# A gated linear attention with a max-out layer behind it: weights in contiguous blocks, groups of two tiles, row moves from another queue, and a new order of the opening

## The chip, the cores and the metric

The kernel runs on one core of a Trainium2 chip. Times are device microseconds of one execution. The time of the kernel before in its first three runs was 207.36 us (median; 206.71 to 207.45). A profile is one such execution recorded by the hardware profiler; its span is from the first to the last instruction.

Ratios are the mean time of one kernel's fast runs over that of the other's of the same rounds, so not quite the ratio of the medians that are quoted beside them. The medians are of all executions and can hold slow ones: two of four in e2s_sync_moves, one each in e2_pool_moves, b2_weights and e7_o_later, and of the kernel before five of seven in the rounds of e6 and e7 (median 209.14; its two fast ones took 207.27 and 205.84). Intervals are 95%. Where an interval lies wholly below 0.98 the text calls the kernel faster; the record classes six of these runs (e2s, b2, e3, e5, e6, e7) as unclear all the same, without a reason.

## The reference

```python
# q, k, v, f_logit: (B=4, H=8, S=768, D=48) float32
f = 1 / (1 + exp(-f_logit))
for t in range(S):                                  # a gated linear attention
    state = f[:, :, t, :, None] * state + k_t (x) v_t
    y[:, :, t] = q_t . state
x = y.transpose(0, 2, 1, 3).reshape(B * S, H * D)   # 3072 x 384
out = maximum(x @ w1, x @ w2) @ w_out               # d_ff = 1024
```

## The kernel before

The sequence is cut into 6 chunks of 128 positions. A *tile* is one chunk of one batch, so there are 24 tiles; each passes through the stages E (logs of the gates), C and X (cumulated sums and their exponentials), M (k and q scaled by them, on GpSimd), V, T (transposes), A (masked products), Y (output and state). The layer behind uses max(a, b) = b + relu(a - b): with wd = w1 - w2 and M2 = w2 @ w_out, the output is relu(x @ wd) @ w_out + x @ M2. Eight *h* pieces make relu(x @ wd) for a group of tiles, and one *o* piece per tile the output.

The attention leaves x transposed, in a layout of two halves of 64 partitions: 48 rows of a head, then 16 rows to be filled from a fourth plane, so that 384 rows fit into three planes of 128. The fill is a DMA from SBUF to SBUF, the *row move*. The rows of w1 and w2 must be in the same order; before, the load puts them there, in pieces of 48 and 16 partitions.

```python
def load(n):                                   # four loads of 192 KB a tile
    ...
        nc.sync.dma_start(out=t, in_=src[b, :, sl, :].rearrange("h p d -> p h d"))

def load_rows(dst, w):                         # rows of w1, w2 straight into their places
    hd = w.rearrange("(h d) f -> d h f", d=D)
    nc.sync.dma_start(out=dst[0:D, :, :], in_=hd[:, 0:6:2, :])
    nc.sync.dma_start(out=dst[DP:DP + D, :, :], in_=hd[:, 1:6:2, :])
    for r in range(2):
        h = 6 + r
        rows = w[h * D:(h + 1) * D, :].rearrange("(k i) f -> i k f", k=KT)
        nc.sync.dma_start(out=dst[r * DP + D:(r + 1) * DP, :, :], in_=rows)
...
def stage_Y_act(n):
    ...
    nc.scalar.copy(xT[c][:, :, b * C:(b + 1) * C], ys.pop(n))
    if b == B - 1:                             # once in four tiles: six row moves
        x = xT[c]
        for r in range(2):
            for i in range(KT):
                nc.sync.dma_start(out=x[r * DP + D:(r + 1) * DP, i, :],
                                  in_=x[r * DP + 16 * i:r * DP + 16 * (i + 1), KT, :])
...
for n in range(5):                             # five tiles ahead
    load(n)
    if n == B - 1:
        load_rows(w2_f, moe_w2); load_rows(w1_f, moe_w1); ...   # then w_out
...                                            # slot n, one for each tile:
    load(n + 5); E(n + 3); A(n); Y(n - 1); C, X, M (n + 2)
    ...                                        # weights are prepared in slots 3, 4, 5
    piece_d; V, T (n + 1); piece_d; piece_o    # two h pieces and one o, if there are any
```

In the profiles the row moves of the sync queue are issued behind the loads that precede them in the code (in e2s_sync_moves below at 85.09 us, after four loads issued from 81.8 to 85.0). Names in the profiles: PEld is TensorE's weight loading, DVE VectorE, POOL GpSimd, SPq and ACTq the issuing of DMAs on the sync queue and on ScalarE's; ft is the loaded gates, kp and qp the scaled k and q, trp and trs their transposes, at_e and at_o the products of A, gT is relu(x @ wd), and wdn and m2n are wd and M2 before they are permuted.

Of the kernel before, what the change touches and what calls it, by code (L numbers as in the profile page):

```python
# [16 lines left out]
def kernel(  # L17
# [17 lines left out]
    nc = tc.nc  # L35
# [9 lines left out]
    NT = B * C  # L45
# [17 lines left out]
    loaded = {}  # L63

    def load(n):
        c, b = divmod(n, B)
        sl = slice(c * C, (c + 1) * C)
        tiles = {}
        for nm, src in (("f", f_logit), ("k", k), ("q", q), ("v", v)):
            t = inp.tile([C, H, D], F32, name=f"{nm}t", tag=f"{nm}t")  # L70
            nc.sync.dma_start(out=t, in_=src[b, :, sl, :].rearrange("h p d -> p h d"))  # L71
            tiles[nm] = t
        loaded[n] = tiles
# [5 lines left out]
    def load_rows(dst, w):  # L79

        hd = w.rearrange("(h d) f -> d h f", d=D)
        nc.sync.dma_start(out=dst[0:D, :, :], in_=hd[:, 0:6:2, :])
        nc.sync.dma_start(out=dst[DP:DP + D, :, :], in_=hd[:, 1:6:2, :])
        for r in range(2):
            h = 6 + r
            rows = w[h * D:(h + 1) * D, :].rearrange("(k i) f -> i k f", k=KT)
            nc.sync.dma_start(out=dst[r * DP + D:(r + 1) * DP, :, :], in_=rows)
# [7 lines left out]
    nc.gpsimd.memset(ones_col, 1.0)  # L95
    NB = 3
    padded = {}
    for nm in ("ell", "qp", "kp", "vb"):
        padded[nm] = []
        for i in range(NB):  # L100
            t = consts.tile([C, H, DP], BF16, name=f"{nm}{i}")
            nc.gpsimd.memset(t, 0.0)
            padded[nm].append(t)
    ut4 = consts.tile([C, NP, C], BF16, name="ut4")
    for j in range(NP):
        nc.gpsimd.tensor_copy(ut4[:, j, :], ut)

    wd = consts.tile([C, KT, d_ff], BF16, name="wd")
    w2b = consts.tile([C, KT, d_ff], BF16, name="w2b")
    wo = consts.tile([C, FG, HD], BF16, name="wo")  # L110
    w2T = consts.tile([C, FG, HD], BF16, name="w2T")
# [128 lines left out]
    def stage_Y_act(n):  # L240
        c, b = divmod(n, B)
        if b == 0:
            xT[c] = xpool.tile([C, NP, NT], BF16, name="xT", tag="xT", bufs=3)
        nc.scalar.copy(xT[c][:, :, b * C:(b + 1) * C], ys.pop(n))  # L244
        if b == B - 1:
            x = xT[c]
            for r in range(2):
                for i in range(KT):
                    nc.sync.dma_start(out=x[r * DP + D:(r + 1) * DP, i, :],  # L249
                                      in_=x[r * DP + 16 * i:r * DP + 16 * (i + 1), KT, :])  # L250


    def piece_d(g, ff):
        if ff == 0:
            gT[g] = xpool.tile([C, FG, NT], BF16, name="gT", tag="gT")
        ps = bank("h")
        for kt in range(KT):
            nc.tensor.matmul(out=ps, lhsT=wd[:, kt, ff * C:(ff + 1) * C], rhs=xT[g][:, kt, :],  # L258
                             start=(kt == 0), stop=(kt == KT - 1))
        nc.scalar.activation(gT[g][:, ff, :], ps, AF.Relu)  # L260

    def piece_o(g, b):
# [7 lines left out]
        return ps  # L270

    def finish_o(g, b, ps):
        ob = opool.tile([C, HD], F32, name="ob", tag="ob")
        nc.vector.tensor_copy(ob, ps)  # L274
        row = b * S + g * C
        nc.sync.dma_start(out=out[row:row + C, :], in_=ob)

    def prep_weights_1():
        nc.vector.tensor_copy(w2b, w2_f)
        nc.gpsimd.tensor_sub(wd, w1_f, w2_f)  # L280
        nc.vector.tensor_copy(wo, wo_f)

    def prep_weights_2():
        for kt in range(KT):
            ps = bank("w2t", BF16).rearrange("p (f r) -> p f r", f=FG)
# [5 lines left out]
    def prep_weights_3():  # L291
        for kt in range(KT):
            ps = bank("m2p")[:, 0:HD]
# [3 lines left out]
            nc.scalar.copy(m2[:, kt, :], ps)  # L297
# [3 lines left out]
    first = {3: prep_weights_1, 4: prep_weights_2, 5: prep_weights_3}  # L301
    queue = []
    for n in range(AHEAD):
        load(n)
        if n == B - 1:
# [84 lines left out]
```

## Time and profile before

| | before |
|---|---|
| time, span | 207.36, 204.9 us |
| TensorE busy (PE) | 141.6 us, 69% |
| first h | 72.8 us |
| last o ends | 201.4 us |
| a full slot (attention, two h, one o) | 5.03 us |

### The profile page before, as it was taken

The page shows a single profiled execution, that of the slowest core. Times are in us where ns is not written, and L with a number is a line of the kernel's source. Part 1 is how long each engine was busy: PE and PEld are TensorE (multiplying, and loading weights), DVE is VectorE, ACT ScalarE, POOL GpSimd, SP SyncE. Part 2 cuts the span into 40 slices and gives each one's busy share as a digit, 9 for nine tenths or more (in the row PEclk, how much of TensorE's full clock was granted, in tenths as well). Part 3 has the DMA queues.
Part 4 walks back from the last instruction along what each step waited for, and adds up shares of the span by engine and source line. Part 5 has one row for each costly group of instructions (what it writes and reads, how often), then busy time and mean ns, then how long its engine had stood idle before and what let it go on. Part 6 is the DMA issues. An engine that isn't in the chain of part 4 may idle for free.

```text
span 204.9 us, 3795 instructions
## 1 busy us (share of the span) xinstructions
PE 141.6 (69%) x1452; PEld 85.7 (42%) x1472; DVE 81.6 (40%) x145; ACT 87.6 (43%) x196; POOL 72.3 (35%) x90
## 2 busy tenths in 40 slices
PE   0257300004464999929999699995999999959993
PEld 0134200002353655614666356663566655515551
DVE  0047500001978346531555426662566554111221
ACT  4333000017552479823666346664466544313400
POOL 8754000003599508640455505554055530000000
PEclk9999999999999799975999979997999999979999
DMA  6999999999999499958699589795891111111122
GB/s 126 189 186 191 162 163 168 228 242 198 186 187 187 72 187 185 171 97 172 141 176 217 116 167 179 150 224 107 168 196 45 58 42 40 45 55 38 55 95 80
DMA packets 106402, 29.15 MB, mean 142 GB/s; under 512 B 100944, under 2 KB 105616, under 8 KB 106384
## 3 DMA queue, kind: packets, MB, share of 16 engines
q1 hardware_dynamic: 106384, 28.91, 77.7%
q8 instruction: 11, 0.18, 0.4%
q14 instruction: 7, 0.06, 0.1%
HBM read 23.59 MB, written 4.72 MB: 138 GB/s over the span
## 4 chain that ended last, share of the span: by engine, by line
PE 52%; issue 19%; SPq 9%; DMA 8%; DVE 5%; ACT 3%; POOL 2%; DVEq 0%; POOLq 0%
PE h L258 15%; PE o L268 13%; PE o L265 5%; SPq L249 5%; PE trp L160 4%; SPq L71 4%; DMA xT<-xT 4%; PE at_e L178 3%; PE y L205 3%; PE y L200 3%; PE m2p L295 2%; DMA ft<-in_f_logit_dram 2%; DMA qt<-in_q_dram 2%; PE cum L127 2%; DVE vb L153 1%
## 5 line engine op out<-in xcount | busy, mean ns | idle before, releaser
L258 PE MATMUL h<-xT,wd 128*128 128x512 bf16 x124 | 41.7, 413 | 12.2 <-DMA xT<-xT 10.3
L260 ACT ACTIVATE gT<-h 128x512 bf16<-128x512 f32 x48 | 28.9, 603 | 31.2 <-PE h L258 30.7
L147 POOL TENSOR_TENSOR kp<-kt,f_inv 128x384 bf16<-128x384 f32 x24 | 24.9, 1037 | 39.6 <-ACT f_inv L140 36.0
L168 DVE COPY trs<-trp 128x1024 bf16<-128x1024 bf16 x24 | 16.6, 691 | 54.3 <-PE trp L160 54.3
L268 PE MATMUL o<-wo,gT 128*128 128x384 bf16 x192 | 35.1, 326 | 0.0
L274 DVE COPY ob<-o 128x384 f32<-128x384 f32 x24 | 13.4, 558 | 52.4 <-PE o L268 52.4
L127 PE MATMUL cum<-ell,ut 128*128 128x384 bf16 x24 | 9.3, 389 | 32.4 <-ACT ell L121 32.4
L120 ACT ACTIVATE tmp_e<-ft 128x384 f32<-128x384 f32 x24 | 12.4, 518 | 42.2 <-DMA ft<-in_f_logit_dram 42.2
L235 POOL TENSOR_TENSOR state<-tmp_s,f_last 128x256 bf16<-128x256 f32 x16 | 10.5, 658 | 53.2 <-DVE tmp_s L234 47.3
L244 ACT CAST xT<-y 128x512 bf16<-128x512 f32 x24 | 14.0, 582 | 29.4 <-PE y L205 29.4
L268 PEld LDWEIGHTS <-gT 128*128 128x128 bf16 x192 | 18.9, 98 | 12.7 <-issue 0.5
L149 POOL TENSOR_TENSOR qp<-qt,f_dec 128x384 bf16<-128x384 f32 x24 | 24.0, 1000 | 0.0
L258 PEld LDWEIGHTS <-wd 128*128 128x128 bf16 x144 | 12.6, 102 | 22.1 <-DMA xT<-xT 14.0
L130 PEld LDWEIGHTS <-ell 128*128 128x128 bf16 x96 | 6.5, 104 | 33.3 <-issue 32.3
L186 DVE TENSOR_TENSOR at_m<-at_e,ut 128x512 bf16<-128x512 f32 x24 | 16.4, 685 | 5.7 <-PE at_o L178 5.7
L178 PE MATMUL at_e<-trs 48*128 48x128 bf16 x96 | 10.7, 240 | 10.7 <-DVE trs L168 10.3
L265 PE MATMUL o<-m,xT 128*128 128x384 bf16 x72 | 16.7, 344 | 0.0
L186 DVE TENSOR_TENSOR at_m<-at_o,ut 128x512 bf16<-128x512 f32 x24 | 16.3, 681 | 0.0
L153 DVE CAST vb<-vt 128x384 bf16<-128x384 f32 x24 | 12.0, 498 | 7.1 <-DMA vt<-in_v_dram 7.1
L178 PEld LDWEIGHTS <-trs 48*128 48x128 bf16 x192 | 6.1, 102 | 18.4 <-DVE trs L168 13.7
L160 PE MATMUL trp<-ident,kp 128*128 128x128 bf16 x96 | 11.1, 249 | 3.1 <-POOL kp L147 3.1
L121 ACT ACTIVATE ell<-tmp_e 128x384 bf16<-128x384 f32 x24 | 12.6, 523 | 0.9
(42 smaller groups left out, 168.5 us busy)
## 6 DMA issues: line engine op xcount, KB each, us to landing
ft<-in_f_logit_dram SPq DMA_DIRECT2D x24, 192.0 KB, 4.0
kt<-in_k_dram SPq DMA_DIRECT2D x24, 192.0 KB, 4.4
qt<-in_q_dram SPq DMA_DIRECT2D x24, 192.0 KB, 4.4
vt<-in_v_dram SPq DMA_DIRECT2D x24, 192.0 KB, 4.2
out_dram<-ob SPq DMA_DIRECT2D x24, 192.0 KB, 2.0
w_f<-in_moe_w_dram SPq DMA_DIRECT2D x4, 576.0 KB, 13.2
wo_f<-in_moe_w_out_dram SPq DMA_DIRECT2D x1, 1536.0 KB, 20.8
w_f<-in_moe_w_dram SPq DMA_DIRECT2D x4, 192.0 KB, 16.0
```

The lines of the kernel that those rows point to most:

```text
L147: nc.gpsimd.tensor_mul(padded["kp"][n % NB][:, :, 0:D], loaded[n]["k"], f_inv.rearrange("p (h d) -> p h d", h=H))
L149: nc.gpsimd.tensor_mul(padded["qp"][n % NB][:, :, 0:D], loaded[n]["q"], f_dec.rearrange("p (h d) -> p h d", h=H))
L153: nc.vector.tensor_copy(padded["vb"][n % NB][:, :, 0:D], loaded[n]["v"])
L160: nc.tensor.transpose(out=ps[:, x, j, :], in_=src[:, 2 * j:2 * j + 2, :].rearrange("p h e -> p (h e)"), identity=ident)
L168: nc.vector.tensor_copy(t, ps)
L178: nc.tensor.matmul(out=ps[r][:, j, :], lhsT=t[rows, 0, j, :], rhs=t[rows, 1, j, :], start=True, stop=True)
L186: nc.vector.tensor_mul(m[:, r], ps[r], ut4)
L244: nc.scalar.copy(xT[c][:, :, b * C:(b + 1) * C], ys.pop(n))
L258: nc.tensor.matmul(out=ps, lhsT=wd[:, kt, ff * C:(ff + 1) * C], rhs=xT[g][:, kt, :], start=(kt == 0), stop=(kt == KT - 1))
L260: nc.scalar.activation(gT[g][:, ff, :], ps, AF.Relu)
L265: nc.tensor.matmul(out=ps, lhsT=xT[g][:, kt, b * C:(b + 1) * C], rhs=m2[:, kt, :], start=(kt == 0), stop=False)
L268: nc.tensor.matmul(out=ps, lhsT=gT[g][:, ff, b * C:(b + 1) * C], rhs=wo[:, ff, :], start=False, stop=(ff == FG - 1))
```

## The change

It has four main parts. (1) w1 and w2 are loaded as they lie, 128 rows at a time, and put in order afterwards by matmuls with 0/1 matrices: 14 for wd, 7 for M2. (2) The layer works on groups of two tiles instead of four, so h matmuls have 256 columns instead of 512 and twice the count. (3) The row moves are two DMAs a group instead of six, issued from ScalarE's queue. (4) The opening has a new order: attention of two tiles, then all weights, then the first group's layer, then the loop; in the loop loads are three tiles ahead instead of five. The full diff also moves the set-up memsets from GpSimd to VectorE and gives xT four buffers instead of three.

```diff
-    def load_rows(dst, w):  ...
+    def load_weights():
+        for dst, w in ((w2_f, moe_w2), (w1_f, moe_w1)):
+            for kt in range(KT):
+                nc.sync.dma_start(out=dst[:, kt, :], in_=w[kt * C:(kt + 1) * C, :])
+        ...                                        # w_out in two halves
+    perm = consts.tile([C, KT, KT, 2, DP], BF16, name="perm")     # built by GpSimd
...
-                for i in range(KT):
-                    nc.sync.dma_start(out=x[r * DP + D:(r + 1) * DP, i, :], ...)
+                rows = x[r * DP:r * DP + D, KT, :]
+                nc.scalar.dma_start(out=x[r * DP + D:(r + 1) * DP, 0:KT, :], in_=rows)
...
+    def weights_w2():
+        for kt in range(KT):
+            nc.scalar.copy(w2b[:, kt, :], w2_f[:, kt, :])
+            ...                                    # 8 transposes, copy to w2T by DVE
+    def weights_wd():
+        for kt in range(KT):
+            nc.vector.tensor_sub(wdn[:, kt, :], w1_f[:, kt, :], w2_f[:, kt, :])
+        ...                                        # 14 matmuls with perm, 6 copies
+    def weights_m2():
+        for h in range(2):
+            nc.scalar.copy(wo[:, half, :], wo_f[:, half, :])
+        ...                                        # 24 matmuls, 7 with perm, 6 copies
...
+    load(0); load(1); load(2, "f"); load(3, "f")
+    load_weights()
+    load(2, "kqv"); load(3, "kqv"); load(4)
+    ...                                            # tiles 0 and 1 up to Y; E, C of 2 and 3
+    weights_w2()
+    weights_wd()
+    do("M", 2)
+    for fp in range(FG // 2):
+        piece_d(0, fp)
+    weights_m2()
+    do("VT", 2); do("M", 3); do("E", 4)
...
+        if 5 <= n + 3 < n_tiles:                   # slot n, from n = 2
+            load(n + 3)
+        A(n); Y(n - 1); C, M (n + 2); piece_d; V, T (n + 1); piece_d; E(n + 3); piece_o
```

More of the change, by code (lines that the diff above doesn't have):

```diff
@@ L44 @@
     KT = HD // C
-    NT = B * C
+    GB = 2
+    NT = GB * C
     n_tiles = nch * B
@@ L60, with load @@
     nc.scalar.preload_act_table_set("natural_log_exp_and_others")
-    loaded = {}
-    def load(n):
+    loaded = {n: {} for n in range(n_tiles)}
+    sources = {"f": f_logit, "k": k, "q": q, "v": v}
+    def load(n, names="fkqv"):
         c, b = divmod(n, B)
-        sl = slice(c * C, (c + 1) * C)
-        tiles = {}
-        for nm, src in (("f", f_logit), ("k", k), ("q", q), ("v", v)):
+        for nm in names:
             t = inp.tile([C, H, D], F32, name=f"{nm}t", tag=f"{nm}t")
-            nc.sync.dma_start(out=t, in_=src[b, :, sl, :].rearrange("h p d -> p h d"))
-            tiles[nm] = t
-        loaded[n] = tiles
+            nc.sync.dma_start(out=t, in_=sources[nm][b, :, c * C:(c + 1) * C, :].rearrange("h p d -> p h d"))
+            loaded[n][nm] = t
     w1_f = wst.tile([C, KT, d_ff], F32, name="w1_f")
@@ L77 @@
     wo_f = wst.tile([C, FG, HD], F32, name="wo_f")
-    def load_rows(dst, w):
-        hd = w.rearrange("(h d) f -> d h f", d=D)
-        nc.sync.dma_start(out=dst[0:D, :, :], in_=hd[:, 0:6:2, :])
-        nc.sync.dma_start(out=dst[DP:DP + D, :, :], in_=hd[:, 1:6:2, :])
-        for r in range(2):
-            h = 6 + r
-            rows = w[h * D:(h + 1) * D, :].rearrange("(k i) f -> i k f", k=KT)
-            nc.sync.dma_start(out=dst[r * DP + D:(r + 1) * DP, :, :], in_=rows)
+    def load_weights():
[3 more added lines that the diff above has]
+        for h in range(2):
+            half = slice(h * FG // 2, (h + 1) * FG // 2)
+            nc.sync.dma_start(out=wo_f[:, half, :],
+                              in_=moe_w_out.rearrange("(j p) m -> p j m", p=C)[:, half, :])
     ut = consts.tile([C, C], BF16, name="ut")
@@ L94 @@
     ones_col = consts.tile([C, 1], BF16, name="ones_col")
-    nc.gpsimd.memset(ones_col, 1.0)
+    nc.vector.memset(ones_col, 1.0)
     NB = 3
     padded = {}
-    for nm in ("ell", "qp", "kp", "vb"):
+    for nm in ("ell", "kp", "qp", "vb"):
         padded[nm] = []
@@ L101 @@
             t = consts.tile([C, H, DP], BF16, name=f"{nm}{i}")
-            nc.gpsimd.memset(t, 0.0)
+            nc.vector.memset(t, 0.0)
             padded[nm].append(t)
@@ L105, with build_perm, sources_of @@
     for j in range(NP):
-        nc.gpsimd.tensor_copy(ut4[:, j, :], ut)
+        nc.vector.tensor_copy(ut4[:, j, :], ut)
+    perm = consts.tile([C, KT, KT, 2, DP], BF16, name="perm")
+    def build_perm():
+        nc.gpsimd.memset(perm, 0.0)
+        for kt in range(KT):
+            for cols, pattern, base in (
+                    (slice(0, D), [[-2 * D, KT], [-D, 2], [-1, D]], kt * C),
+                    (slice(D, DP), [[-1, KT], [-D, 2], [-KT, DP - D]], kt * C - 2 * KT * D)):
+                part = perm[:, kt, :, :, cols]
+                nc.gpsimd.affine_select(out=part, in_=part, compare_op=mybir.AluOpType.not_equal,
+                                        fill=1.0, base=base, pattern=pattern, channel_multiplier=1)
+    def sources_of(i):
+        return sorted({2 * D * i // C, (2 * D * (i + 1) - 1) // C, KT - 1})
+    w2b = wst.tile([C, KT, d_ff], BF16, name="w2b")
+    wdn = wst.tile([C, KT, d_ff], BF16, name="wdn")
+    w2T = wst.tile([C, FG, HD], BF16, name="w2T")
+    m2n = wst.tile([C, KT, HD], BF16, name="m2n")
     wd = consts.tile([C, KT, d_ff], BF16, name="wd")
-    w2b = consts.tile([C, KT, d_ff], BF16, name="w2b")
     wo = consts.tile([C, FG, HD], BF16, name="wo")
-    w2T = consts.tile([C, FG, HD], BF16, name="w2T")
     m2 = consts.tile([C, KT, HD], BF16, name="m2")
@@ L240, in stage_Y_act, with piece_d @@
     def stage_Y_act(n):
-        c, b = divmod(n, B)
+        g, b = divmod(n, GB)
         if b == 0:
-            xT[c] = xpool.tile([C, NP, NT], BF16, name="xT", tag="xT", bufs=3)
-        nc.scalar.copy(xT[c][:, :, b * C:(b + 1) * C], ys.pop(n))
-        if b == B - 1:
-            x = xT[c]
+            xT[g] = xpool.tile([C, NP, NT], BF16, name="xT", tag="xT", bufs=4)
+        nc.scalar.copy(xT[g][:, :, b * C:(b + 1) * C], ys.pop(n))
+        if b == GB - 1:
+            x = xT[g]
             for r in range(2):
-                for i in range(KT):
-                    nc.sync.dma_start(out=x[r * DP + D:(r + 1) * DP, i, :],
-                                      in_=x[r * DP + 16 * i:r * DP + 16 * (i + 1), KT, :])
-    def piece_d(g, ff):
-        if ff == 0:
-            gT[g] = xpool.tile([C, FG, NT], BF16, name="gT", tag="gT")
-        ps = bank("h")
-        for kt in range(KT):
-            nc.tensor.matmul(out=ps, lhsT=wd[:, kt, ff * C:(ff + 1) * C], rhs=xT[g][:, kt, :],
-                             start=(kt == 0), stop=(kt == KT - 1))
-        nc.scalar.activation(gT[g][:, ff, :], ps, AF.Relu)
+                rows = x[r * DP:r * DP + D, KT, :]
+                nc.scalar.dma_start(out=x[r * DP + D:(r + 1) * DP, 0:KT, :], in_=rows)
+    def piece_d(g, fp):
+        if fp == 0:
+            gT[g] = xpool.tile([C, FG, NT], BF16, name="gT", tag="gT", bufs=3)
+        ps = bank("h").rearrange("p (f t) -> p f t", f=2)
+        for f in range(2):
+            ff = 2 * fp + f
+            for kt in range(KT):
+                nc.tensor.matmul(out=ps[:, f, :], lhsT=wd[:, kt, ff * C:(ff + 1) * C],
+                                 rhs=xT[g][:, kt, :], start=(kt == 0), stop=(kt == KT - 1))
+        nc.scalar.activation(gT[g][:, 2 * fp:2 * fp + 2, :], ps, AF.Relu)
     def piece_o(g, b):
@@ L269, in piece_o @@
                              start=False, stop=(ff == FG - 1))
-        return ps
-    def finish_o(g, b, ps):
         ob = opool.tile([C, HD], F32, name="ob", tag="ob")
         nc.vector.tensor_copy(ob, ps)
-        row = b * S + g * C
+        c, bb = divmod(g * GB + b, B)
+        row = bb * S + c * C
         nc.sync.dma_start(out=out[row:row + C, :], in_=ob)
-    def prep_weights_1():
-        nc.vector.tensor_copy(w2b, w2_f)
-        nc.gpsimd.tensor_sub(wd, w1_f, w2_f)
-        nc.vector.tensor_copy(wo, wo_f)
-    def prep_weights_2():
+    def weights_w2():
         for kt in range(KT):
+            nc.scalar.copy(w2b[:, kt, :], w2_f[:, kt, :])
             ps = bank("w2t", BF16).rearrange("p (f r) -> p f r", f=FG)
@@ L289, in prep_weights_2 @@
             nc.vector.tensor_copy(w2T[:, :, kt * C:(kt + 1) * C], ps)
-    def prep_weights_3():
+    def weights_wd():
         for kt in range(KT):
-            ps = bank("m2p")[:, 0:HD]
+            nc.vector.tensor_sub(wdn[:, kt, :], w1_f[:, kt, :], w2_f[:, kt, :])
+        for h in range(2):
+            half = slice(h * d_ff // 2, (h + 1) * d_ff // 2)
+            for i in range(KT):
+                ps = bank("wdp")
+                ks = sources_of(i)
+                for kt in ks:
+                    nc.tensor.matmul(out=ps, lhsT=perm[:, kt, i].rearrange("p r d -> p (r d)"),
+                                     rhs=wdn[:, kt, half], start=(kt == ks[0]), stop=(kt == ks[-1]))
+                if i == 1:
+                    nc.vector.tensor_copy(wd[:, i, half], ps)
+                else:
+                    nc.scalar.copy(wd[:, i, half], ps)
+    def weights_m2():
+        for h in range(2):
+            half = slice(h * FG // 2, (h + 1) * FG // 2)
+            nc.scalar.copy(wo[:, half, :], wo_f[:, half, :])
+        for kt in range(KT):
+            ps = bank("m2n")[:, 0:HD]
             for ff in range(FG):
@@ L296, in prep_weights_3, with do, next_piece @@
                                  start=(ff == 0), stop=(ff == FG - 1))
-            nc.scalar.copy(m2[:, kt, :], ps)
-    AHEAD = 5
-    first = {3: prep_weights_1, 4: prep_weights_2, 5: prep_weights_3}
-    queue = []
-    for n in range(AHEAD):
-        load(n)
-        if n == B - 1:
-            load_rows(w2_f, moe_w2)
-            load_rows(w1_f, moe_w1)
-            nc.sync.dma_start(out=wo_f, in_=moe_w_out.rearrange("(j p) m -> p j m", p=C))
-    def ok(n):
-        return 0 <= n < n_tiles
-    def next_piece(n, kind):
+            nc.scalar.copy(m2n[:, kt, :], ps)
+        for i in range(KT):
+            ps = bank("m2p")[:, 0:HD]
+            ks = sources_of(i)
+            for kt in ks:
+                nc.tensor.matmul(out=ps, lhsT=perm[:, kt, i].rearrange("p r d -> p (r d)"),
+                                 rhs=m2n[:, kt, :], start=(kt == ks[0]), stop=(kt == ks[-1]))
+            nc.vector.tensor_copy(m2[:, i, :], ps)
+    AHEAD = 5
+    done = set()
+    steps = {
+        "E": stage_E, "M": stage_M, "V": stage_V,
+        "C": lambda n: (stage_C(n), stage_X(n)),
+        "T": lambda n: (stage_T_pe(n), stage_T_dve(n)),
+        "A": lambda n: (stage_A_pe(n), stage_A_dve(n)),
+        "Y": lambda n: (stage_Y_pe(n), stage_Y_act(n), stage_D_pe(n), stage_D_dve(n)),
+    }
+    def do(names, n):
+        for nm in names:
+            if 0 <= n < n_tiles and (nm, n) not in done:
+                done.add((nm, n))
+                steps[nm](n)
+    load(0)
+    load(1)
+    load(2, "f")
+    load(3, "f")
+    load_weights()
+    load(2, "kqv")
+    load(3, "kqv")
+    load(4)
+    do("E", 0)
+    do("E", 1)
+    for n in range(2):
+        do("CM", n)
+    for n in range(2):
+        do("VT", n)
+    build_perm()
+    do("A", 0)
+    do("A", 1)
+    for n in range(2):
+        do("E", n + 2)
+    for n in range(2):
+        do("Y", n)
+    for n in range(2, 4):
+        do("C", n)
+    weights_w2()
[4 more added lines that the diff above has]
+    weights_m2()
+    do("VT", 2)
+    do("M", 3)
+    do("E", 4)
+    queue = [("o", 0, b) for b in range(GB)]
+    def next_piece(kind):
         for i, (kd, g, j) in enumerate(queue):
@@ L317, in next_piece @@
                 if kd == "o" and any(p[0] == "d" and p[1] == g for p in queue):
-                    return None
-                return queue.pop(i)
-        return None
-    slot = -3
-    while slot < n_tiles + 2 or queue:
-        n = slot
-        if n % B == 1 and 4 < n <= n_tiles + 1:
-            g = (n - 5) // B
-            queue += [("d", g, ff) for ff in range(FG)] + [("o", g, b) for b in range(B)]
-        if ok(n + AHEAD) and n + AHEAD >= AHEAD:
-            load(n + AHEAD)
-        if ok(n + 3):
-            stage_E(n + 3)
-        if ok(n):
-            stage_A_pe(n)
-            stage_A_dve(n)
-        if ok(n - 1):
-            stage_Y_pe(n - 1)
-            stage_Y_act(n - 1)
-            stage_D_pe(n - 1)
-            stage_D_dve(n - 1)
-        if ok(n + 2):
-            stage_C(n + 2)
-            stage_X(n + 2)
-            stage_M(n + 2)
-        if n in first:
-            first[n]()
-        p = next_piece(n, "d")
-        if p:
-            piece_d(*p[1:])
-        if ok(n + 1):
-            stage_V(n + 1)
-            stage_T_pe(n + 1)
-            stage_T_dve(n + 1)
-        p = next_piece(n, "d")
-        if p:
-            piece_d(*p[1:])
-        p = next_piece(n, "o")
-        if p:
-            finish_o(*p[1:], piece_o(*p[1:]))
-        slot += 1
+                    return
+                queue.pop(i)
+                (piece_d if kind == "d" else piece_o)(g, j)
+                return
+    n = 2
+    while n < n_tiles + 2 or queue:
+        if n % GB == 1 and 3 < n <= n_tiles + 1:
+            g = (n - 3) // GB
+            queue += [("d", g, fp) for fp in range(FG // 2)] + [("o", g, b) for b in range(GB)]
+        if 5 <= n + 3 < n_tiles:
+            load(n + 3)
+        do("A", n)
+        do("Y", n - 1)
+        do("C", n + 2)
+        do("M", n + 2)
+        next_piece("d")
+        do("V", n + 1)
+        do("T", n + 1)
+        next_piece("d")
+        do("E", n + 3)
+        next_piece("o")
+        n += 1
 _INS = ['q', 'k', 'v', 'f_logit', 'moe_w1', 'moe_w2', 'moe_w_out']
```

## The prediction

> **What bounds the kernel now.** I read four views of the profile of before, coarse to fine. First the page's span in 40 slices of 5.1 us (digits: tenths busy):
>
> ```profile
> ## 2 busy tenths in 40 slices
> PE   0257300004464999929999699995999999959993
> PEclk9999999999999799975999979997999999979999
> DMA  6999999999999499958699589795891111111122
> ```
>
> TensorE (PE) is nearly full from the 15th slice on, with four holes; before that it is mostly idle while DMA is full. So there are two regimes: an opening that is not TensorE's, and a TensorE-bound rest with holes. The whole-span share (PE 69%) hides both. Next, stretches of 1 us (last three columns: granted clock, DMA share, GB/s):
>
> ```profile
> 30.00:31.00 1.00, 0.00 (x0) 0.00 (x0) 0.00 (x0) 0.00 (x0) 0.00 (x0) 1.00 0.96 147
> 41.00:42.00 1.00, 0.00 (x0) 0.00 (x0) 0.00 (x0) 0.00 (x0) 0.00 (x0) 1.00 1.07 373
> 52.00:53.00 1.00, 1.00 (x16) 0.63 (x11) 1.00 (x4) 0.00 (x0) 1.00 (x2) 1.00 1.43 185
> ```
>
> The first is w1/w2 arriving in pieces of 48 and 16 partitions, the second w_out arriving on all 128, the third the 192-byte rows of q, k, v, f. From 25 to 45 us no compute engine does anything: the next tile's f is queued behind 4.7 MB of weights. Third, the chain that ended last (start us, duration us, what), with a hole and a full slot (one tile's worth of every stage):
>
> ```profile
> 20.03 27.31 issue
> ...
> 87.02 0.81 SPq L249
> 87.88 0.59 SPq L249
> 88.52 1.59 SPq L249
> 90.15 1.84 DMA xT<-xT
> 92.04 0.61 PE h L258
> 92.66 0.61 PE h L258
> ...
> 98.50 0.34 PE y L200 x8
> 98.84 0.34 PE y L205 x8
> 99.94 0.38 PE h L258
> 100.32 0.45 PE trp L160 x8
> 100.77 0.65 PE h L258 x3
> 101.42 0.49 PE o L265 x3
> 101.90 1.30 PE o L268 x8
> 103.53 0.34 PE y L200 x8
> ```
>
> A full slot takes 103.53 - 98.50 = 5.03 us, all TensorE: 1.79 for o, 1.30 for two h pieces, so 1.94 for attention. The hole is the six row moves of x, issued one after another on the sync queue behind loads that wait for buffers; h waits for the last. The timeline of that queue shows the next one:
>
> ```profile
> 112.40 3.89 SPq L249 DMA_DIRECT2D xT<-xT  x6
> ```
>
> **Account of before.** TensorE is at work from 72.8 us (first h) to 201.4 us (last o), 128.6 us. Its work in there is 24 o at 1.79 (43.0), 24 pairs of h at 1.30 (31.2) and about 18.4 tiles of attention at 1.94 (35.7), together 109.9. So holes and the slow matmuls after them cost 128.6 - 109.9 = 18.7 us. The end (copy of ob, last store) takes 204.9 - 201.4 = 3.5.
>
> [...] The trace has 143 to 197 in this phase, against 373 for all partitions[...] Trace: 0.65 us for three of 512 columns, 217 each[...]; 256 columns are then estimated at 109, so smaller groups cost TensorE nothing. [...] Trace: 24 transposes in 2.58 us at 60 us, 107 ns each, against 56 (0.45/8) later[...]
>
> **The change part by part.**
>
> *Weights.* 4.72 MB at about 350 GB/s instead of 28 us for them: 13.5 us. The first ten loads (two tiles and two f) run at the old pace of about 1.05 us each, to 13 us; the weights are in by about 27, where they now land at 45.
>
> *Opening, by engine.* It becomes a chain of computations. The transposes of tile 1 end near 14.3 us (as in the trace's first tiles, with both tiles' transposes ahead of the first A). Then DVE: trs to 15.1, four masks at 0.68 to 17.7; Y of tile 1 and its ScalarE copy to 19.1; two row moves issued by ScalarE, 0.5 each as on the sync queue, 20.1; exponentials of tiles 2 and 3, 1.13 each, 22.4. ScalarE then casts w2: its groups cost about 0.18 us + 0.83 ns per column (4 columns 181 ns, 384 490, 512 603), so 1.03 each for three, 25.5. Transposes and w2T copy, 27.3. Subtractions on DVE: at 1.05 ns per column (256 take 416, 512 take 685) 1.2 each, 30.9. Permuting wd: 14 matmuls of 512 columns, half of them cold, 4.8, to 35.7. h of group 0, 24 of 256 columns, 38.3; last ReLU 39.0. Casts of w_out on ScalarE, two of 1.46, 41.9. M2: 24 matmuls of 163 ns, most after the second cast, 45.2; copy, 7 permuting matmuls, copies, 47.7; V and T of tile 2 and their copy; A of tile 2 at **49 us**. The three permutation matrices on GpSimd (about 3.5 us) are done by 17, beside other work.
>
> *TensorE work left from there.* 24 o (43.0), 11 groups of h at 2.6 (28.6), 22 tiles at 1.94 less what is already done of 2 and 3 (41.3): **112.9 us**. A last group of two tiles instead of four also shortens the tail's last dependent piece.
>
> *Holes.* The row moves lose their queue: issued right after the copy of y, 0.5 + 1.9 us to land, needed over 3 us later. The 18.7 us should go.
>
> *New waits.* (a) In every second slot ScalarE issues two row moves (0.9 to 1.2 us) between the copy of y and the exponentials. In a full slot of before, copy ends at +1.72, second ReLU at +3.96. Shifted, it ends near +4.9; the o that follows in that slot needs it at 3.16 + 0.49 + 6 x 0.163 = +4.63. So about 0.35 us in ten slots: **4 us** with the same for late loads. (b) Loads are now three tiles ahead, each behind the previous output store on the in-order queue: f is issued at +1.1 and lands 3.1 to 4.0 us later, just when it is wanted. In slots 2 to 5, which have less TensorE work, I put down **2 us**.
>
> Sum: 49.0 + 112.9 + 4 + 2 + 3.4 = 171.3 us of span; the timed median is 2.4 above the span of before (207.36 against 204.9): 173.7. I say 173.5.
>
> **Rivals.** *Weights hidden anyway or still slow:* at the old 165 GB/s they would land at 42, w_out would hold M2, A of tile 2 moves to 54 or so: 179. For it: nothing but caution; against it: 373 GB/s in the trace for this shape. *DMA becomes the bound:* a tile's loads take 4.2 us at 187 GB/s and its store 0.6, 4.8 of a 5.03 slot, and the slack of five tiles is gone. If every f is late by 0.5 us, 18 slots give +9: 182. Against it: in full slots of before the sync queue waits for ob some 2 us each, so it keeps up. *ScalarE becomes the bound:* at 0.8 us or more per issue the even slots grow by about 1 us: 180. *Everything fits, ScalarE's issue is cheap and PE is warm earlier:* start at 45, no stalls: 163.5. *The two-tile groups cost weight loads:* against it, 128-column transposes already run at 56 ns with a load each.
>
> **Range and chances.** The start is uncertain by 4, the stalls by 5 each way: 164 to 182. Even the worst sum of rivals, near 190, is 8% faster. Faster 0.985, same 0.01, slower 0.005.
>
> **What would show it.** GB/s above 300 in the weight stretch, ending before 30 us. First full-rate slot near 50 us; if A of tile 2 comes after 54 or before 45 the opening's chain is wrong, and the step is found by where the w2 casts, subtractions and w_out casts end. No TensorE idle over 1 us on xT; slots of 5.0 and 5.4 us in turn, the longer with o waiting for gT. If instead cum waits for ell after ft, rival DMA is right. A span above 182 means a wait of over 0.8 us in every slot.

Measured in the trace of before: 143 to 197 GB/s for the pieces of w1 and w2 against 373 for w_out; 217 ns for a matmul of 512 columns, from which 109 for 256 is an estimate; and transposes of 107 ns at 60 us and 56 later, both while the granted clock read 1.00. "Cold" and "warm" name these two rates; that half of the permuting matmuls would be cold was the author's estimate. So were the 350 GB/s for the weights (from w_out, 335 over 39 to 43 us), the 3.5 us for the permutation matrices (the trace of the change has 3.2, from 13.3 to 16.5 us), and the 0.6 us of a store (in the trace of before, after the loads have ended, DMA has a share of 0.11 over 5.0 us in which one store passes, so 0.55 us).

## More of the kernel before

The views that carry the argument stand in the prediction. Two groups of instructions sum them up; the columns are line, engine, operation, output and inputs, shapes and count, then busy us and mean ns of one, then the idle time of the engine just before and what ended it.

```profile
L258 PE MATMUL h<-xT,wd 128*128 128x512 bf16 x124 | 41.7, 413 | 12.2 <-DMA xT<-xT 10.3 <-issue 0.8
L120 ACT ACTIVATE tmp_e<-ft 128x384 f32<-128x384 f32 x24 | 12.4, 518 | 42.2 <-DMA ft<-in_f_logit_dram 42.2
```

The first group is TensorE's layer, which waited 10.3 us for row moves. The second is stage E, where ScalarE (ACT) waited 42.2 us for the gates, nearly all of it in the opening while the weights were coming in.

## The result, and the profile after

| | before | after |
|---|---|---|
| time, median | 207.04 us | 180.78 us (179.95 to 181.04, 4 runs) |
| ratio | | 0.874, interval 0.868 to 0.880 |
| span of the profile | 204.9 us | 178.1 us |
| TensorE busy | 141.6 us, 69% | 144.2 us, 81% |
| A of tile 2, from which on the loop runs | | 50.3 us |
| last o ends | 201.4 us | 174.8 us |

The changed kernel is 13% faster. The forecast of 173.5 us lay 7.3 us too low; its range of 164 to 182 holds the result. The page's 40 slices, now 4.45 us each:

```profile
PE   0157361877979579999999999999999999999992
PEclk9999999996999957999999999999999999999999
DMA  6999999990006999689799997999999986111112
```

TensorE (PE) is full from the 17th slice on, and the four holes of before are gone. Two things are new: DMA does next to nothing in slices 10 to 12 (1 GB/s from 40 to 53 us), and TensorE has a weak spot in slices 14 to 16, with a lower clock (PEclk, 0.50 to 0.57 from 62 to 69 us).

Stretches of 1 us (length, then busy time of PE, PEld, DVE, ACT, POOL, then granted clock, DMA share and GB/s) show the weights on their way, the idle DMA, and the weak spot:

```profile
18.00:19.00 1.00, 1.00 (x18) 0.66 (x15) 0.42 (x1) 0.59 (x1) 0.00 (x0) 1.00 1.01 406
41.00:42.00 1.00, 0.61 (x4) 0.26 (x3) 0.00 (x0) 1.00 (x1) 0.00 (x0) 0.78 0.00 0
65.00:66.00 1.00, 1.00 (x9) 0.87 (x8) 0.00 (x0) 0.42 (x3) 1.00 (x2) 0.50 1.31 201
```

The contiguous blocks run at 406 GB/s, where the pieces ran at 141 to 197 (before, 25 to 39 us). At 65 us TensorE works at half clock (0.50).

**The opening**, from the timeline (start us, duration us, engine, line, what, count, and in brackets the idle time before it with its releaser):

```profile
26.54 5.09 DVE L305 TENSOR_TENSOR wdn<-w_f 128x1024 bf16<-128x1024 f32 x3
39.29 2.83 ACT L322 CAST wo<-wo_f 128x1536 bf16<-128x1536 f32 x2
42.17 4.77 PE L326 MATMUL m2n<-wo,w2T 128*128 128x384 bf16 x20 [0.56 <-ACT wo L322]
50.30 0.23 PE L194 MATMUL at_e<-trs 48*128 48x128 bf16 x1 [1.21 <-DVE trs L184]
```

The halves of w_out had landed 8.5 and 9.9 us after issues at 14.4 and 15.7, so by 26 us. Their cast starts at 39.3 because ScalarE reaches it then, not because it waits for data. The steps of the predicted chain against the trace (end times, us):

| step | predicted | trace |
|---|---|---|
| weights landed | 27 | 25.6 |
| casts of w2 | 25.5 | 24.8 |
| w2T copied | 27.3 | 26.6 |
| subtractions | 30.9 | 31.6 |
| permuted wd | 35.7 | 36.1 |
| h of group 0 | 38.3 | 38.8 |
| casts of w_out | 41.9 | 42.1 |
| M2 before permuting | 45.2 | 46.9 |
| A of tile 2 starts | 49 | 50.3 |

**The ramp.** Slot lengths from one A to the next: slots 2 to 6 took 3.28, 3.74, 3.63, 6.75 and 5.91 us, 23.3 together, for 16.7 us of TensorE work (2.8, 3.73, 1.94, 3.24, 5.03, from the pieces that they hold). The chain that ended last shows part of why (start us, duration us, what; pieces under 0.1 us left out):

```profile
54.47 3.67 DMA ft<-in_f_logit_dram
58.16 0.53 ACT tmp_e L136
58.74 0.41 issue
59.15 0.58 ACT xT L260
59.75 0.58 ACTq L265
60.37 3.76 DMA xT<-xT
64.18 1.46 PE h L275 x6
```

The load of tile 6's gates is issued only at 54.47, after the first output store, although DMA had been idle since 40. ScalarE waits for it, and behind it in ScalarE's order stand the copy of y and the row move. The move then takes 3.76 us. The first h of the loop starts at 64.18 and is slow: 1.46 us for six matmuls, 0.68 later.

**The full slots** alternate: 5.05, 5.51, 5.05, 5.46, 5.05, 5.45 from slot 7 on. Of the longer ones two later reach 5.59 and 5.73. The chain through one of them, slot 10 (pieces under 0.1 us left out):

```profile
90.35 0.59 ACT xT L260
90.96 0.56 ACTq L265
91.56 0.60 ACTq L265
92.27 0.49 ACT f_inv L156
92.76 0.38 ACT f_dec L157
93.21 0.50 ACT gT L277
93.76 0.99 PE o L285 x4
```

The two row moves hold ScalarE for 0.56 + 0.60 us; its exponentials and ReLUs come that much later, and the last part of o waits for gT.

### The profile page after: what moved, and what is told of

It reads as the page before. It is cut to its first block, busy times and chain, and to the rows that moved or that the text cites. A ratio compares the mean times of both kernels' runs of the same rounds, so it can differ in the third digit from the quotient of the medians.

```text
span 178.1 us, 4161 instructions
## 1 busy us (share of the span) xinstructions
PE 144.2 (81%) x1636; PEld 97.6 (55%) x1637; DVE 88.8 (50%) x168; ACT 95.4 (54%) x205; POOL 64.1 (36%) x79
## 4 chain that ended last, share of the span: by engine, by line
PE 43%; DMA 27%; ACT 10%; DVE 7%; SPq 6%; ACTq 3%; issue 2%; DVEq 0%
DMA ft<-in_f_logit_dram 14%; PE h L275 12%; PE o L285 12%; DMA kt<-in_k_dram 5%; DMA xT<-xT 5%; SPq L71 5%; PE o L282 4%; DMA w_f<-in_moe_w_dram 3%; DVE wdn L305 3%; PE m2n L326 3%; ACTq L265 3%; PE trp L176 2%; PE wdp L312 2%; ACT tmp_e L136 2%; PE y L221 2%
## 5 line engine op out<-in xcount | busy, mean ns | idle before, releaser
L163 POOL TENSOR_TENSOR kp<-kt,f_inv 128x384 bf16<-128x384 f32 x24 | 25.8, 1076 | 51.1 <-ACT f_inv L156 41.0
L275 PE MATMUL h<-xT,wd 128*128 128x256 bf16 x288 | 39.5, 279 | 0.5 <-DMA xT<-xT 0.4
L285 PE MATMUL o<-wo,gT 128*128 128x384 bf16 x192 | 38.0, 327 | 0.5 <-ACT gT L277 0.2
L288 DVE COPY ob<-o 128x384 f32<-128x384 f32 x24 | 13.3, 556 | 45.3 <-PE o L285 41.0
L277 ACT ACTIVATE gT<-h 128x512 bf16<-128x512 f32 x48 | 27.9, 609 | 11.1 <-PE h L275 10.7
L275 PEld LDWEIGHTS <-wd 128*128 128x128 bf16 x288 | 26.4, 99 | 4.2 <-DMA xT<-xT 0.7
L285 PEld LDWEIGHTS <-gT 128*128 128x128 bf16 x192 | 17.3, 98 | 17.3 <-ACT gT L277 7.2
L165 POOL TENSOR_TENSOR qp<-qt,f_dec 128x384 bf16<-128x384 f32 x24 | 24.7, 1031 | 0.3 <-DMA qt<-in_q_dram 0.3
L184 DVE COPY trs<-trp 128x1024 bf16<-128x1024 bf16 x24 | 16.5, 689 | 14.6 <-PE trp L176 14.6
L251 POOL TENSOR_TENSOR state<-tmp_s,f_last 128x256 bf16<-128x256 f32 x16 | 10.6, 662 | 36.5 <-DVE tmp_s L250 36.5
L136 ACT ACTIVATE tmp_e<-ft 128x384 f32<-128x384 f32 x24 | 12.7, 531 | 16.4 <-DMA ft<-in_f_logit_dram 16.4
L156 ACT ACTIVATE f_inv<-cum 128x384 f32<-128x384 f32 x24 | 11.8, 491 | 16.9 <-POOL state L251 8.4
L202 DVE TENSOR_TENSOR at_m<-at_e,ut 128x512 bf16<-128x512 f32 x24 | 16.4, 682 | 2.2 <-PE at_o L194 2.1
L282 PE MATMUL o<-m,xT 128*128 128x384 bf16 x72 | 15.6, 326 | 0.0
L146 PEld LDWEIGHTS <-ell 128*128 128x128 bf16 x96 | 6.1, 100 | 12.3 <-issue 10.9
L157 ACT ACTIVATE f_dec<-cum 128x384 f32<-128x384 f32 x24 | 11.7, 488 | 0.0
```

Of the source, the lines that this page charges most:

```text
L136: nc.scalar.activation(tmp, ft, AF.Exp, bias=0.0, scale=-1.0)
L163: nc.gpsimd.tensor_mul(padded["kp"][n % NB][:, :, 0:D], loaded[n]["k"], f_inv.rearrange("p (h d) -> p h d", h=H))
L165: nc.gpsimd.tensor_mul(padded["qp"][n % NB][:, :, 0:D], loaded[n]["q"], f_dec.rearrange("p (h d) -> p h d", h=H))
L184: nc.vector.tensor_copy(t, ps)
L202: nc.vector.tensor_mul(m[:, r], ps[r], ut4)
L275: nc.tensor.matmul(out=ps[:, f, :], lhsT=wd[:, kt, ff * C:(ff + 1) * C], rhs=xT[g][:, kt, :], start=(kt == 0), stop=(kt == KT - 1))
```

## The experiments

Eleven kernels ran, all with correct results. In the table, "before" is the median of the kernel before in the same rounds.

| run | what | time | before | ratio (interval) |
|---|---|---|---|---|
| e1_ahead5 | change, loads five ahead | 178.15 | 207.06 | 0.863 (0.858 to 0.867) |
| e2_pool_moves | change, row moves from GpSimd | 176.47 | 207.06 | 0.852 (0.847 to 0.858) |
| e4_old_weights | change, old weight load, no permutation | 181.84 | 207.06 | 0.880 (0.874 to 0.886) |
| b1_moves_act | before, row moves as changed | 191.7 | 207.06 | 0.927 (0.923 to 0.932) |
| e3_both | e1 and e2 | 175.17 | 206.1 | 0.850 (0.846 to 0.854) |
| e5_order | e3 and a shorter opening | 162.73 | 206.1 | 0.791 (0.787 to 0.795) |
| e2s_sync_moves | change, row moves on the sync queue | 200.39 | 206.1 | 0.962 (0.950 to 0.973) |
| b2_weights | before, contiguous weights, permuted | 193.83 | 206.1 | 0.938 (0.928 to 0.947) |
| e6_order_alone | change, shorter opening only | 169.51 | 209.14 | 0.821 (0.811 to 0.830) |
| e7_o_later | e5, no o in slot 2 | 162.33 | 209.14 | 0.785 (0.773 to 0.798) |
| b3_weights_moves | b1 and b2 | 184.16 | 207.19 | 0.887 (0.878 to 0.896) |

The theory after the result: the opening is a chain of computations for which the weights are in time; the ramp is lost to late loads; the even slots are lost to ScalarE's issuing of row moves; and of the gain most comes from the row moves and the weights, each through a queue that stood in the way. The rivals are named with each run.

### e1_ahead5: are the late loads the loss in the ramp?

```diff
     load(4)
+    load(5)
+    load(6)
...
-        if 5 <= n + 3 < n_tiles:
-            load(n + 3)
+        if 7 <= n + 5 < n_tiles:
+            load(n + 5)
```

> The changed kernel with loads five tiles ahead instead of three (tiles 5 and 6 before the loop, tile n + 5 in slot n). Theory L (late loads: each f queues behind the last output store, and behind it ScalarE's copy of y and the row moves): slots 4 to 6, which took 16.3 us for 10.2 us of TensorE work, fall to 11 to 12.5 us, idle of ScalarE on ft from 16.4 us to under 3, time 175 to 176.5 us; every second slot stays at 5.45. Rival M (the row moves themselves, 0.6 us each to issue on ScalarE and 3.7 us to land): slots 4 to 6 stay above 15 us and the time stays within 1 us of 180.8.

Measured: 178.15 us, 2.6 less than the change. Slots 2 to 6 took 21.3 us instead of 23.3; slots 4 to 6 took 14.2, so the expected 11 to 12.5 was missed, and so was the time of 175 to 176.5. ScalarE's wait for ft fell from 16.4 to 6.4 us. The even slots stayed at 5.46. So late loads are a real but smaller part of the ramp; the rest stays. Later in the run two slots got longer: slot 19 took 5.84 us, in which h waited 0.65 us for a DMA, and slot 20 took 6.40, in which the issue of one row move held ScalarE for 1.55 us instead of 0.6. Slots 7 to 21 took 80.6 us, against 80.0 in the change. Why that issue took so long is not shown.

### e2_pool_moves: is ScalarE's issuing the loss in the even slots?

```diff
-                nc.scalar.dma_start(out=x[r * DP + D:(r + 1) * DP, 0:KT, :], in_=rows)
+                nc.gpsimd.dma_start(out=x[r * DP + D:(r + 1) * DP, 0:KT, :], in_=rows)
```

> The changed kernel with the row moves issued by GpSimd instead of ScalarE. Theory A (the 1.2 us of issue on ScalarE delays the second ReLU, for which o waits in every second slot): these slots fall from 5.45 to 5.05 to 5.1 us, no wait of o's weight loads for gT (7.2 us now), time 176 to 177.5 us; slots 4 to 6 stay near 16 us. Rival (the even slots are long for another reason, the DMA or PSUM banks, or GpSimd now delays kp and qp instead): even slots stay at 5.4 or more, time 180 or above.

Measured: 176.47 us, as theory A said. The wait of o's weight loads for gT, 7.2 us in the change, is no longer among the waits, and from slot 14 to 18 every slot is 5.05 to 5.10 us. Slots 8, 10 and 12 fell less, to 5.22, 5.38 and 5.17: there the chain runs through gates that land late (ScalarE waited 20.6 us for them in all, 16.4 in the change), and with loads five ahead (e3) these slots are 5.05 too. The span is 4.0 us shorter, of which 1.6 lie in the opening (A of tile 2 at 48.7: ScalarE, which does not issue moves there either, begins the casts of w2 1.3 us earlier, and the subtractions take 4.3 us instead of 5.1), 0.4 in the ramp and 2.2 in slots 7 to 21 (77.7 us instead of 80.0). So issuing on ScalarE cost about as much in total as was foreseen for the even slots, but half of it elsewhere.

### e4_old_weights: what are the contiguous weights worth here?

```diff
-            for kt in range(KT):
-                nc.sync.dma_start(out=dst[:, kt, :], in_=w[kt * C:(kt + 1) * C, :])
+            hd = w.rearrange("(h d) f -> d h f", d=D)
+            nc.sync.dma_start(out=dst[0:D, :, :], in_=hd[:, 0:6:2, :])
+            nc.sync.dma_start(out=dst[DP:DP + D, :, :], in_=hd[:, 1:6:2, :])
+            ...                     # and the two pieces of 16 rows; no perm matmuls at all
```

> The changed kernel with w1 and w2 loaded as before (pieces of 48 and 16 partitions, already permuted) and no permuting matmuls. Theory C (the opening is a chain of computations, and the fast loads only pay for the permutation): w_out lands near 41 us instead of 27, but 14 + 7 permuting matmuls and 9 copies fall away, A of tile 2 comes at 49 to 53 us instead of 50.3 and the time is 180 to 183.5 us. Rival W (the contiguous loads are what shortened the opening): A of tile 2 at 58 us or later, time 188 or more.

Measured: 181.84 us, and A of tile 2 at 51.3. The last of the weights, w_out, lands at 38.6 us instead of 25.6, and yet the opening is only 1.0 us longer. But loads are on its chain here, which they are not in the change: VectorE waits for w1 before the first subtraction, until 33.5 us.

```profile
DVE wd L310 <- DMA w_f<-in_moe_w_dram: 4.9, 1, 4.9
```

So the run shows the balance that theory C named, and not that loads don't count: in this order the subtractions end 5.4 us earlier with contiguous blocks (31.6 against 37.0), and permuting matmuls and copies pay most of that away again. The intervals of the two ratios (0.868 to 0.880 and 0.874 to 0.886) overlap, so even the sign of the 1 us is not certain from the times alone.

### b1_moves_act: the row moves alone, in the kernel before

```diff
-                for i in range(KT):
-                    nc.sync.dma_start(out=x[r * DP + D:(r + 1) * DP, i, :],
-                                      in_=x[r * DP + 16 * i:r * DP + 16 * (i + 1), KT, :])
+                nc.scalar.dma_start(out=x[r * DP + D:(r + 1) * DP, 0:KT, :],
+                                    in_=x[r * DP:r * DP + D, KT, :])
```

(The 32 rows of w1 and w2 that they meet are read in the matching order.)

> The kernel before with one part of the change alone: the row moves of x as two DMAs from ScalarE's queue instead of six from the sync queue (the 32 rows of w1 and w2 that they meet are read in the matching order). My account of before put 18.7 us on holes at these moves and the slow matmuls after them. If so, the time falls to 189 to 194 us and no wait of h on xT is above 1 us. Rival (the moves are late because the DMA engines are busy, whoever issues them): waits of h on xT of 2 us and more stay, time 201 or above.

Measured: 191.7 us, 15.4 less than before, inside the expected 189 to 194. Of the waits on row moves this line is all that is left:

```profile
PEld L257 <- DMA xT<-xT: 0.4, 1, 0.4
```

It reads: weight loads of h waited for moves 0.4 us in total, once. Before it was 10.3 us for the matmuls alone. Slots are 5.04 us, every fourth 5.30, which is the issuing on ScalarE again.

### e2s_sync_moves: is it the number of moves or the queue?

```diff
-                nc.scalar.dma_start(out=x[r * DP + D:(r + 1) * DP, 0:KT, :], in_=rows)
+                nc.sync.dma_start(out=x[r * DP + D:(r + 1) * DP, 0:KT, :], in_=rows)
```

> The changed kernel with its two row moves put back on the sync queue. Theory Q (what cost the time in the kernel before is the place in the queue: a move issued there stands behind the four loads of its slot, to about +5 us, and lands near +8, when h wants it at +6.4): every second slot gets a wait of h on xT of 1 to 2 us, time 186 to 196 us. Rival (six moves of 0.6 us each were the trouble, two are few enough): time 176 to 180 us.

Measured: 200.39 us (its two fast runs 197.04 and 199.5). The direction of theory Q is right and the size was underestimated: it had 186 to 196. Matmuls of h waited 14.7 us for moves and their weight loads 12.5; before, with six moves for each group of four tiles, it was 10.3 and 14.0. The timeline of the sync queue and of TensorE in one such slot:

```profile
85.09 1.54 SPq L265 DMA_DIRECT2D xT<-xT  x2
88.76 0.81 PE L275 MATMUL h<-xT,wd 128*128 128x256 bf16 x6 [1.43 <-DMA xT<-xT]
```

The moves are issued after the four loads of their slot (81.8 to 85.0), and TensorE stands for 1.43 us. After such waits h also took 1.44 us for six instead of 0.82 (at 66.5 us, where the page's slice has a granted clock of 0.5, and at 165.8, where it is 0.7 from 166.0 on), with slots up to 10.6 us. Two moves on this queue are as bad as six: it is the place in the queue. Without the new queue the whole change would have been worth about 4%.

### b2_weights: the contiguous weights alone, in the kernel before

```diff
-        hd = w.rearrange("(h d) f -> d h f", d=D)
-        ...
+        for kt in range(KT):
+            nc.sync.dma_start(out=dst[:, kt, :], in_=w[kt * C:(kt + 1) * C, :])
...
+        # prep_weights_2: the 14 permuting matmuls of wd; prep_weights_3: the 7 of M2
```

> The kernel before with one part alone: w1 and w2 in contiguous blocks, permuted by 0/1 matmuls, order of the opening and row moves as before. Theory C' (there the order makes the opening wait for the weights, so faster weights count in full, though they counted for only 1 us in the changed order): f of tile 4 lands about 11 us earlier, time 195 to 200 us. Rival (the permutation costs what the loads bring): 204 us or more.

Measured: 193.83 us, 12.3 less than before. Stage E of tile 4 starts at 33.5 us instead of 45.4. The time is below the expected 195 to 200. But the 12 us are not all the opening's. Part of what stage E gains is spent on permuting, and the first h comes at 66.4 us instead of 72.6, so 6 us earlier. Much of the rest is that h waits less for row moves, which this part did not touch: 7.7 us for the matmuls, before it was 10.3, and 4.6 us for their weight loads instead of 14.0.

```profile
66.36 0.81 PE L270 MATMUL h<-xT,wd 128*128 128x512 bf16 x3
PE h L270 <- DMA xT<-xT: 7.7, 6, 3.0
```

The next run, without these waits, puts the worth of the weights in this order at about 8 us. In the changed order it is about 1 (e4).

### b3_weights_moves: are these two parts the whole gain?

The edit is that of b1 and b2 together.

> The kernel before with two parts of the change, the contiguous weights and the row moves from ScalarE's queue, but with its own order of the opening, its groups of four tiles and loads five ahead. One part alone gave ratios of 0.9375 and 0.9272. If they are separate, 0.9375 x 0.9272 = 0.869 and 177 to 182 us, as much as the whole change: the new order and the groups of two tiles then bring nothing of their own. If the change needs its new order to profit, 185 us or more.

Measured: 184.16 us, ratio 0.887 (0.878 to 0.896), between the two theories: the gains do not quite multiply to 0.869, and the change's 0.874 is 0.013 better. Against b1 the weights bring 7.5 us here (medians), where alone they brought 12.3: part of b2's gain was shorter waits for row moves, which b1 removes anyway. The new order and the groups of two together are worth roughly 3 us, net of the shorter lead of the loads. The two were not separated.

### e3_both

The edit is that of e1 and e2 together.

> Loads five ahead and row moves from GpSimd together. If late loads and ScalarE's issue are separate losses, the gains add: 180.8 - 2.6 - 4.3, so 173 to 175 us; slots 4 to 6 at 12 us or less. If both removed the same wait (ScalarE late with the copy of y), the sum gives 176 to 177 us, no better than the row moves alone.

Measured: 175.17 us. The time fits the additive 173 to 175 better than 176 to 177, at its edge, but the statement about slots 4 to 6 was wrong: they took 15.5 us, not 12. The h of slot 5 waited 1.48 us for its row move and then took 1.44 us for six, in a slice of the page with a granted clock of 0.5. What did get better is the rest: slots 7 to 21 took 76.6 us, 1.2 over their work. In the change they were 4.5 over.

### e5_order: shorten the opening's chain

```diff
+    weights_sub()          # the three subtractions, now ahead of the casts of w2
     weights_w2()
     weights_wd()
     do("M", 2)
+    do("M", 3)
+    weights_wo()           # the two casts of w_out, by DVE instead of ScalarE
     for fp in range(FG // 2):
         piece_d(0, fp)
+    do("VT", 2)
     weights_m2()
-    do("VT", 2)
-    do("M", 3)
```

(On top of e3_both.)

> As e3_both, with the opening's chain shortened: the three subtractions before the casts of w2 (DVE idles there from 19 to 24 us), w_out cast by DVE instead of ScalarE behind the ReLUs, V and T of tile 2 before M2. Theory C (the opening is a chain of computations, each step of it counts): A of tile 2 comes at 40 to 44 us instead of about 49 and the time is 165 to 168.5 us. Rival (something else gates tile 2, its loads or GpSimd's kp and qp): A of tile 2 after 47 us, time within 1.5 us of e3_both.

Measured: 162.73 us, 12.4 less than e3_both, which is more than expected. The timeline:

```profile
18.93 3.49 DVE L305 TENSOR_TENSOR wdn<-w_f 128x1024 bf16<-128x1024 f32 x3
28.31 2.62 DVE L310 CAST wo<-wo_f 128x1536 bf16<-128x1536 f32 x2
36.70 0.23 PE L194 MATMUL at_e<-trs 48*128 48x128 bf16 x1
```

A of tile 2 comes at 36.7 instead of 49.1, the same 12.4 us earlier. This shows theory C directly: nothing but the order and the engine of a few instructions was changed, and the weights arrive as before. The subtractions take 3.49 us here and 5.09 in the change, where GpSimd's kp and qp of tiles 2 and 3 ran beside them.

### e6_order_alone: is that gain there without the other two?

The same edit on the change itself, with row moves on ScalarE and loads three ahead.

> The changed kernel with the shortened opening alone; row moves on ScalarE and loads three ahead as in the change. If the three losses are separate, it gains what it gained beside the other two (175.2 - 162.7 = 12.4 us): 167 to 170 us, every second slot still about 5.45. Rival (started 12 us earlier, the loads no longer keep up, because DMA must now bring the same tiles in less time): slots of 5.6 us and more with ScalarE waiting for ft, time 172 us or above.

Measured: 169.51 us, inside 167 to 170. The even slots from 8 to 18 are still 5.46 to 5.89 us. Starting 11 us earlier did not make the loads the bound: ScalarE waits for ft as long as in the change, 16.4 us.

### e7_o_later: fill the empty slot of the ramp

```diff
-        next_piece("o")
+        if n > 2:
+            next_piece("o")
```

(On top of e5_order.)

> As e5_order, with no o piece in slot 2, so that the two o of group 0 fall into slots 3 and 4. Theory H (in the ramp slots 4 to 6 are 14.7 us for 10.2 us of work because TensorE has little to do in slot 4, waits, and then runs at half clock): slot 4's wait is filled, no half clock near 50 us, slots 2 to 6 take 1 to 3 us less than the 21.7 us now, time 160 to 162 us. Rival (the wait in slot 5 is for the row move, whatever fills slot 4): no gain, 162.5 us or more.

Measured: 162.33 us. In the trace theory H is right: slots 2 to 6 take 20.7 us instead of 21.7, and the granted clock stays at 1.00 between 40 and 60 us, where e5_order had 0.74 from 50 to 55. The first h of slot 5 still waits 1.19 us for its row move, as the rival said; what is gone is the half clock after it. In the time, which lies between the two expectations, with intervals of 0.787 to 0.795 and 0.773 to 0.798, the gain is not told from none. The best kernel is one of these two, at 0.79 of before, ahead of the change's 0.874.

## Why the prediction was right or wrong

**Right.** The opening is a chain of computations and not of loads: A of tile 2 at 50.3 against 49. In the trace of the change no step of it waits for weights, and e5 showed the cause by moving instructions alone. Inside it two terms were too small and others too large. The three subtractions were put at 1.2 us each and took 1.22, 2.01 and 2.02 (5.1 together). The last twenty M2 matmuls were put at 3.3 us, warm, and took 4.77, about half of them while the granted clock was 0.50 to 0.52 (42 to 45 us; 1.00 from 45 to 47), after waits of 2.04 and 0.56 us for casts.

The holes of before: 18.7 us were to go. b1 took them away alone and gained 15.4; in the change no hole of that kind is left (h waited 0.4 us for moves, its weight loads 0.7).

The even slots: 0.35 us was expected in ten slots, because the second ReLU comes too late for o. The trace has 0.40 to 0.46 in most of them, by exactly that chain, and e2 removed its wait for gT. The issues had been put at 0.5 us each "as on the sync queue", where their median was 0.59; on ScalarE it was 0.60. The whole term "4 us with the same for late loads" measured 4.5 us in slots 7 to 21.

Smaller groups cost TensorE nothing: six matmuls of 256 columns take 0.66 us in the chain, as three of 512 did.

**Wrong.** The step that failed is the last term of the new waits: "In slots 2 to 5, which have less TensorE work, I put down 2 us". It measured 6.6 us for slots 2 to 6 (23.3 for 16.7 of work). The mechanism named there, a gate load issued late behind the output store, is in the chain, but e1 shows that it accounts for only some 2 us. What the step left out:

- The row move took 3.7 us to land (median of 24, 24 KB each), where I had taken 1.9 from the moves of 16 KB in the trace of before. With ScalarE late, the first h of the loop had no slack for it. The page of the experiment with the moves on GpSimd has 3.6, so this is not ScalarE's doing.
- A slot's length is not its TensorE work when that is small. Slot 4 has 1.94 us of it and took 3.63; with the loads in time (e1) it still took 2.98, a chain of short steps on DVE and ScalarE.
- TensorE then ran at half clock from 62.0 to 68.9 us (granted clock 0.51 in that stretch, 1.00 before and after). Two h groups and the transposes between them took 3.6 us instead of 1.8. I had named the clock for the opening's matmuls and not carried it into the ramp. e7 gives TensorE more work there and does not see the half clock (1.00 from 40 to 60 us).

The sum again: 49.0 was 50.3 (+1.3); 2 was 6.6 (+4.6); 4 was 4.5 for slots 7 to 21 and 0.5 more in the tail (+1.0); the end 3.3 (-0.1). That is the difference of 6.8 us between 171.3 and the span of 178.1. The rest of the 7.3 is the rounding of 173.7 to 173.5 and the span's distance to the median, 2.7 instead of 2.4 (both profiled executions were faster than their medians, so these distances are larger than the 1.9 between each one's own time and span).

The account was also silent on one thing that the experiments brought out: it credited the shorter opening to the weights. In the changed order they contributed 1 us net of the permuting (e4). In the order of e5 they should be worth more, because its subtractions start at 18.9 us and those of e4 could not before 33.5; e5 with the old loads was not run.

**Open.** What the groups of two tiles bring by themselves, apart from the new order, was not tried. How the 4.6 us of the ramp divide between late ScalarE, slow moves and the clock is only bounded by e1, e3 and e7, which each touch more than one.

## What to carry to other kernels

A transfer that is needed soon should not be put behind long loads on their queue: here the same two moves cost about 18 us more on the sync queue than on ScalarE's (fast runs), and another 4 us less on an engine with time to spare. Before a load is made faster, ask what is waiting at its end: here a chain of casts and copies was, the faster loads brought 1 us net, and reordering the chain alone brought 11 to 12 us. When the stages of a pipeline start, count the latency of each step and TensorE's clock, not only the work per slot.

## What the traces measured of the hardware

- The engine that issued the row moves decided the time: 200.4 us with the moves on the sync queue, 180.8 on ScalarE's, 176.5 on GpSimd's. On the sync queue a move was held up by the loads ahead of it (moves issued at 85.1 us behind loads from 81.8 on). Issuing occupied a compute engine: 0.56 to 0.64 us for each move of 24 KB on ScalarE.
- A small move from SBUF to SBUF beside the loads took, from issue to landing, a median of 1.9 us before (16 KB, sync queue), 2.9 in e2s_sync_moves (24 KB, sync queue), 3.7 in the change (24 KB, ScalarE's queue; up to 5.8) and 3.6 in e2_pool_moves (24 KB, GpSimd's queue). The runs do not separate size, queue and load.
- In the ramp of the change the granted clock fell from 1.00 to 0.50 at 62.0 us after gaps of only 1.11 and 0.79 us; in the 4 us before the fall TensorE was busy 2.11. That so little activity was the reason is inferred.
- In the change two of the three subtractions on DVE took 2.0 us, and GpSimd's kp and qp beside them 2.1, 1.6 and 1.9 instead of 1.0. The first, also beside kp, took 1.22, as all three did in e4_old_weights; in e5_order the three took 3.49 together. What slowed the two is not shown.
